# Four attention scores in flight instead of three in the first 60 units, and the bit moves of odd heads placed later

## The chip, the cores and the metric

The kernel runs on one core of one Trainium2 chip. The metric is the time of one execution on the device, in microseconds, the median of the runs; smaller is better. A core has five engines with a queue of instructions each: TensorE (PE in the profile; its weight loads are PEld), VectorE (DVE), ScalarE (ACT), GpSimd (POOL) and SyncE (SP), which issues most of the transfers.

## What is computed

Attention with hashed buckets (4 batches, 8 heads, 768 positions, head dimension 64), and behind it a two-layer network with SiLU on the 3072 tokens (512 to 2048 to 512). Cut to what matters:

```python
q_bits = (einsum('bhsd,dk->bhsk', q, proj) > 0)      # 6 bits; the same for k
mask = q_bucket[:, :, :, None] == k_bucket[:, :, None, :]
scores = where(mask, q @ k.T / 8, -1e9)
attn = exp(scores - max); attn = attn / sum(attn)
x = (attn @ v)  as (3072, 512)
h = x @ w_in; out = (h * sigmoid(h)) @ w_out
```

## The kernel before

The 32 heads are taken as 16 pairs, and a head as nine *units* (`NU`), so there are 288 units. A unit is one score tile of 128 keys by 512 queries, or two halves of 256, in one PSUM bank. Its life: `score(w)` issues one or two matmuls (L381) with K-transposed as weights, ScalarE applies the exponential and writes `u` (L384), and `av(w)` multiplies: four small matmuls (L413) with the parts of `u` as weights and the values `vv` (65 columns, the last of ones, for the row sums) as the moving side. The mask is part of the score: rows 64 to 76 of the operand tiles `QKA` and `QKB` hold the bucket bits (rows 0 to 12 for the odd head), so that the contraction itself puts pairs of unequal buckets far below zero.

Before a pair can be scored it has to be prepared, and for pairs 1 to 5 this is done so:

- `t_unit(p, i)`, i = 0 to 2: four transposes on TensorE into a PSUM tile `tp_ps` (L199), which VectorE copies to `qk32` in SBUF (L201). The third copy completes the pair.
- `cast_unit(p, par)`: GpSimd scales `qk32` into `QKA` (even head) or `QKB` (odd head) in fp16 (L265).
- `proj_halves(p)` (pairs 1 to 3): four projections on TensorE into `bp_ps` (L315), of which VectorE makes `bits` by a comparison (L317).
- `bits_halves(p, par)`: four small moves on VectorE (L332, L335) from `bits` into `QKA` or `QKB`, one for each half of q and of k.

Pairs 4 and 5 use `proj_unit` and `bits_unit` (L295, L301, L359); pair 0 has functions of its own (`t_first`, `proj_first`: L212, L239). `v_unit` prepares the values on GpSimd. At the end of a head VectorE takes the reciprocal of the row sums and scales the output into `x_pr` (L432, L433). `x_unit` transposes `x_pr` to `xT`, by a transfer, or for pairs 2 and 3 on TensorE (L445). The network of the first batch (L478, L488, L491) is mixed in from unit 65 on.

The order of all this is written out by hand. `plan(w, fn)` puts a piece of preparation ahead of unit w, and the main loop runs, for each w: what is planned for w, then pieces of the network if any, then `av(w)`, then `score(w + LEAD)` with `LEAD = 3`. Each engine takes its instructions in this order. So three units are scored ahead of the product that is being issued.

PSUM has eight banks, handed out from rings by tags: "s" with three buffers for scores, "m" with three for transposes, projections and, later, the hidden layer, and "o" with two for the outputs of heads. A new tile of a ring waits until the tile three (or two) turns before it has been read. The pool of `u` has six buffers.

Of the kernel before, what the change touches and what calls it, by code (L numbers as in the profile page):

```python
# [9 lines left out]
F32 = mybir.dt.float32  # L10
# [7 lines left out]
def kernel(  # L18
# [15 lines left out]
    P = 128  # L34
# [23 lines left out]
    ps = ctx.enter_context(tc.tile_pool(name="ps", bufs=1, space=bass.MemoryType.PSUM))  # L58
# [7 lines left out]
    def load_qk(p):  # L66
        b, h0 = p // 4, 2 * (p % 4)
        for n, src in (("q", q), ("k", k)):
            t = ld.tile([P, NJ, 2, D], F32, tag=f"ld{n}", name=f"{n}_sb")
            nc.sync.dma_start(  # L70
                out=t, in_=src[b, h0 : h0 + 2].rearrange("h (p t) d -> p t h d", p=P))
            qk_sb[p, n] = t
# [25 lines left out]
    def load_v(p, heads=slice(0, 2)):  # L98
        b, h0 = p // 4, 2 * (p % 4)
        if p not in v_sb:  # L100
            v_sb[p] = vld.tile([P, 2, NJ * D], F32, tag="ldv", name="v_sb")
        nc.sync.dma_start(
            out=v_sb[p][:, heads],
            in_=v[b, h0 : h0 + 2][heads].rearrange("h (p t) d -> p h (t d)", p=P))
# [87 lines left out]
    def t_unit(p, i):  # L192
        if i == 0:
            qk32[p] = t32.tile([P, 2 * S], F32, tag="qk32", name="qk32")
        tp = ps.tile([P, 512], F32, tag="m", name="tp_ps", bufs=3)
        for j in range(4):
            n, t = divmod(4 * i + j, NJ)
            src = qk_sb[p, "qk"[n]]
            nc.tensor.transpose(tp[:, j * P : (j + 1) * P],  # L199
                                src[:, t].rearrange("p h d -> p (h d)"), ident)  # L200
        nc.vector.tensor_copy(out=qk32[p][:, 512 * i : 512 * (i + 1)], in_=tp)  # L201
# [60 lines left out]
    def cast_unit(p, par):  # L262
        sl = p % NSL
        dst, rows = ((QKA[sl], slice(0, 64)), (QKB[sl], slice(64, 128)))[par]
        nc.gpsimd.tensor_scalar(out=dst[rows, :], in0=qk32[p][rows, :],  # L265
                                scalar1=CS, scalar2=1.0,
                                op0=ALU.mult, op1=ALU.mult)

    def v_unit(p, heads=(0, 1)):
        for i in heads:  # L270
            h = 2 * p + i
            vv, vs = VV[h % NVS], VS[p % (NVS // 2)]
            src = v_sb[p][:, i, :].rearrange("p (t d) -> p t d", d=D)
            nc.gpsimd.tensor_copy(out=vv[:, :, 0:D], in_=src)  # L274
            sa = nrm.tile([P, 3, D], F32, tag="vsa", name="vsa")
            nc.gpsimd.tensor_tensor(out=sa, in0=src[:, 0:3], in1=src[:, 3:6], op=ALU.add)  # L276
            sb = nrm.tile([P, D], F32, tag="vsb", name="vsb")
            nc.gpsimd.tensor_tensor(out=sb, in0=sa[:, 0], in1=sa[:, 1], op=ALU.add)
            nc.gpsimd.tensor_tensor(out=vs[:, i, 0:D], in0=sb, in1=sa[:, 2], op=ALU.add)
# [27 lines left out]
    def proj_halves(p):  # L307


        bt = btp.tile([P, 3, P + 2], F16, tag="bits", name="bits")  # L310
        bp = ps.tile([P, 512], F32, tag="m", name="bp_ps", bufs=3)
        for c in range(4):
            half, n = divmod(c, 2)
            x0 = n * S + half * HS
            nc.tensor.matmul(bp[32 * c : 32 * c + 32, 0:HS], pw[:, 0:32],  # L315
                             qk32[p][:, x0 : x0 + HS], start=True, stop=True)
        nc.vector.tensor_scalar(out=bt[:, :, 0:P],  # L317
                                in0=bp[:, 0:HS].rearrange("d (x c) -> d x c", c=P),
                                scalar1=sc[:, 0:1], scalar2=sc[:, 1:2],
                                op0=ALU.is_gt, op1=ALU.subtract)  # L320
        bits[p] = bt

    def bits_halves(p, par):
        t, r0 = ((QKA[p % NSL], 64), (QKB[p % NSL], 0))[par]
        for c in range(4):
            half, n = divmod(c, 2)
            x0 = n * S + half * HS
            nr = NR if par else NBIT + 1
            r = slice(32 * c, 32 * c + nr)
            dst = t[r0 : r0 + nr, x0 : x0 + HS].rearrange("d (x c) -> d x c", c=P)  # L330
            if n == 1 and par == 1:
                nc.vector.tensor_scalar(out=dst, in0=bits[p][r, :, 0:P],  # L332
                                        scalar1=sc[r, 2:3], scalar2=None, op0=ALU.mult)
            else:
                nc.vector.tensor_copy(out=dst, in_=bits[p][r, :, 0:P])  # L335
# [27 lines left out]

    NU = 9
    LEAD = 3
    ut = {}

    def parts(w):
        h, r = divmod(w, NU)
        jp, j = divmod(r, 3)  # L370
        if j == 1:
            return h, [(2 * jp, 512, 256, 0), (2 * jp + 1, 512, 256, 256)]
        return h, [(2 * jp + j // 2, 0, 512, 0)]

    def score(w):
        h, pts = parts(w)
        p, par = divmod(h, 2)
        t = QKA[p % NSL] if par == 0 else QKB[p % NSL]
        sp = ps.tile([P, 512], F32, tag="s", name="s_ps", bufs=LEAD)
        for jt, c0, n, o0 in pts:  # L380
            nc.tensor.matmul(sp[:, o0 : o0 + n], t[:, S + jt * P : S + (jt + 1) * P],  # L381
                             t[:, c0 : c0 + n], start=True, stop=True)
        u = upl.tile([P, 512], F16, tag="u", name="u")
        nc.scalar.activation(out=u, in_=sp, func=AF.Exp, scale=ESC)  # L384
        ut[w] = u
# [68 lines left out]
    def flush():  # L454
        for fn in after:
            fn()
        after.clear()
# [150 lines left out]
    def moe_head():  # L608
        order = [0, 1, 2, 3, 6, 4] if len(late) == 13 else range(min(6, len(late)))
        units = [late[i] for i in order]  # L610
        late[:] = [u for i, u in enumerate(late) if i not in order]
        return units
# [221 lines left out]
    NW = NH * NU  # L834
# [32 lines left out]
    def plan(w, fn):  # L867
        at.setdefault(w, []).append(fn)
# [2 lines left out]
    plan(1, second_head)  # L871
    plan(3, lambda: nc.gpsimd.memset(QKA[2][64:128, :], 0.0))
    for i in range(3):
        plan(4 + 2 * i, lambda i=i: t_unit(1, i))
    for i in range(2):
        plan(8, lambda i=i: cast_unit(1, i))
        plan(8, lambda i=i: v_unit(1, (i,)))
    plan(10, lambda: proj_halves(1))
    for i in range(2):
        plan(11 + i, lambda i=i: bits_halves(1, i))  # L880
        plan(0, lambda p=2 + i: load_qk(p))
        plan(3 + i, lambda p=2 + i: load_v(p))

    for p, steps, wp in ((2, (14, 17, 20), 24), (3, (28, 31, 34), 41)):
        for i in range(3):
            plan(steps[i], lambda p=p, i=i: t_unit(p, i))
        for par in range(2):
            plan(steps[2], lambda p=p, par=par: cast_unit(p, par))
            plan(wp + 1 + 2 * par, lambda p=p, par=par: bits_halves(p, par))
        plan(wp, lambda p=p: proj_halves(p))  # L890
    for i in range(2):
        for j in range(2):
            plan(18 + 9 * i + 2 * j, lambda p=2 + i, j=j: v_unit(p, (j,)))
        plan(21 + i, lambda p=4 + i: load_qk(p))
# [10 lines left out]
    for Q in range(2, NQUAD):  # L905
# [8 lines left out]
        wp = w0 + {3: 24, 4: 24, 2: 24}.get(Q, 20)  # L914
# [26 lines left out]
    credit = 0.0  # L941
    scoring = True
    in_head = False
    for w in range(LEAD):
        score(w)
    for w in range(NW):
        flush()
        for fn in at.pop(w, []):
            fn()
        if w % BST == 1:  # L950
            moeq.extend(moe_head())
        if w == BST + 5 or w % BST == 11 and w > 2 * BST:
            credit = 0.5
            moeq.extend(moe_list(w // BST - 1))
        keep = 3 if w >= NW - 12 else 0
        left = BST - w % BST
        n = -(-(len(moeq) - keep) // left) if len(moeq) > keep else 0
        in_head = w > 2 * BST and w % BST < 11 or w >= NW - 20
        ahead = BST + 9 < w < 2 * BST
        credit += max(len(moeq) + ahead - keep, 0) / left  # L960
        skip = credit < 0.999 or w % QST in ((20, 21) if w > 2 * BST else (24, 25))
        if w > 2 * BST and w % BST < 11:
            skip = w % BST in (0, 2, 5, 7, 10)
        if n == 1 and len(moeq) - keep < left and skip:
            n = 0
        credit -= n
        if w == BST + 9:
            n = 1
        for _ in range(n):
            moeq.popleft()()  # L970
        av(w)
        if w + LEAD < NW:
            score(w + LEAD)
    while moeq:
        flush()
        moeq.popleft()()
# [35 lines left out]
```

The softmax here doesn't subtract the row's maximum and nothing guards it: scores larger than these inputs give would overflow.

## Time and profile before

| | |
|---|---|
| time, median of 3 runs | 292.36 us (292.26 to 292.48) |
| span of the profiled execution | 290.9 us |
| TensorE busy | 286.3 us, 98% |
| ScalarE busy | 224.5 us, 77% |
| GpSimd busy | 209.4 us, 72% |
| VectorE busy | 201.9 us, 69% |
| first score | 8.79 us |
| product of unit 59 | 42.52 us |

A line of the timeline reads: start, duration, engine, line of the code, operation, out<-in by tile names, how many instructions are merged in it, and in brackets the idle time before it with what ended it. In lists of waits the first number is the total in us, then how often, then the longest. `QKA` is `qka` in the profile and `bp_ps`, `tp_ps`, `s_ps` and `o_ps` are the PSUM tiles. Units up to 59, where the change works, are the first 43 us.

### The profile page before, as it was taken

The numbers are of one execution on the slowest core, as the hardware profiler recorded it, in microseconds if no ns is written. First come the engines' busy times: TensorE is split into PE (matmuls) and PEld (weight loads), VectorE is DVE, ScalarE is ACT, GpSimd is POOL, SyncE is SP. The second block draws the span as 40 slices with busy tenths as digits, with TensorE's granted clock in tenths as the row PEclk, the third lists the DMA queues.
The fourth block names the chain that finished last, engine by engine and source line by source line (L and its number), as shares of the span: only waits on it lengthen the run. The fifth ranks groups of instructions, "written<-read, shape, count | busy, mean of one in ns | idle before, by whom it ended". The sixth has DMA issues, their size and how long they took to land.

```text
span 290.9 us, 7761 instructions
## 1 busy us (share of the span) xinstructions
PE 286.3 (98%) x2934; PEld 196.8 (68%) x2934; DVE 201.9 (69%) x402; ACT 224.5 (77%) x428; POOL 209.4 (72%) x243
## 2 busy tenths in 40 slices
PE   8999999999999999999999999999999999999995
PEld 3676775555667655567666888656668887666885
DVE  5888879899968564855798447975556758777333
ACT  5899998998988686877887877877888865888400
POOL 8779999478998975999357992579999762654400
PEclk9999999999999999999999999999999999999999
DMA  7999997959989439882189325313120211201114
GB/s 201 244 253 193 206 151 121 232 93 179 175 129 206 99 66 195 185 161 54 48 187 125 66 68 114 107 46 38 37 47 0 65 23 60 75 3 36 38 66 134
DMA packets 105861, 32.91 MB, mean 113 GB/s; under 512 B 90912, under 2 KB 105312, under 8 KB 105824
## 3 DMA queue, kind: packets, MB, share of 16 engines
q1 hardware_dynamic: 101296, 28.13, 48.3%
q0 software_dynamic: 4224, 4.19, 9.5%
q8 instruction: 23, 0.38, 0.6%
q10 hardware_dynamic: 304, 0.10, 0.1%
q14 instruction: 14, 0.11, 0.1%
HBM read 27.27 MB, written 6.29 MB: 115 GB/s over the span
## 4 chain that ended last, share of the span: by engine, by line
PE 96%; ACT 2%; issue 1%; DVE 0%; POOL 0%; DVEq 0%; ACTq 0%; POOLq 0%
PE h_ps L478 21%; PE s_ps L381 20%; PE o_ps L530 15%; PE o_ps L413 13%; PE h_ps L689 6%; PE o_ps L796 6%; PE o_ps L560 5%; PE bp_ps L295 3%; ACT u L384 2%; PE tp_ps L199 2%; PE warm_ps L125 1%; PE bp_ps L315 1%; PE tp_ps L212 1%; PE bp_ps L239 1%; PE o_ps L404 0%
## 5 line engine op out<-in xcount | busy, mean ns | idle before, releaser
L384 ACT ACTIVATE u<-s_ps 128x512 f16<-128x512 f32 x288 | 157.4, 612 | 27.1 <-PE s_ps L381 26.8
L413 PEld LDWEIGHTS <-u 128*128 128x128 f16 x1152 | 67.2, 98 | 38.2 <-ACT u L384 9.7
L413 PE MATMUL o_ps<-vv,u 128*128 128x65 f16 x1152 | 82.4, 194 | 0.3
L478 PE MATMUL h_ps<-xT,win 128*128 128x512 f16 (+1 forms) x384 | 75.1, 326 | 0.0
L491 DVE SCALAR_TENSOR_TENSOR g<-th,h_ps 128x512 f16<-128x512 f32 x72 | 48.4, 680 | 36.6 <-ACT th L488 36.1
L381 PE MATMUL s_ps<-qkb 128*128 128x512 f16 x192 | 53.0, 326 | 0.0
L381 PE MATMUL s_ps<-qka 128*128 128x512 f16 x192 | 52.6, 326 | 0.1
L488 ACT ACTIVATE th<-h_ps 128x512 f32<-128x512 f32 x72 | 44.4, 617 | 10.3 <-PE h_ps L478 7.1
L478 PEld LDWEIGHTS <-win 128*128 128x128 f16 x384 | 37.5, 98 | 17.9
L530 PEld LDWEIGHTS <-g 128*128 128x128 f16 x336 | 32.8, 98 | 6.8
L433 POOL TENSOR_TENSOR x_pr<-osum,rec 128x384 f16<-128x384 f32 x23 | 20.0, 872 | 21.6 <-DVE rec L432 20.4
L265 POOL TENSOR_SCALAR qka<-qk 64x1536 f16<-64x1536 f32 x15 | 21.9, 1463 | 14.9 <-DVE qk L260 11.5
L265 POOL TENSOR_SCALAR qkb<-qk 64x1536 f16<-64x1536 f32 x15 | 22.0, 1469 | 1.2
L530 PE MATMUL o_ps<-wt,g 128*128 128x256 f16 x168 | 21.8, 273 | 0.0
L530 PE MATMUL o_ps<-wout,g 128*128 128x256 f16 x168 | 21.4, 273 | 0.0
L513 POOL TENSOR_TENSOR g<-g 128x1024 f16<-128x1024 f16 x7 | 15.2, 2192 | 7.8 <-PE o_ps L530 7.8
L276 POOL TENSOR_TENSOR vsa<-v_sb 128x192 f32<-128x192 f32 x32 | 18.9, 590 | 0.0
L274 POOL CAST vv<-v_sb 128x384 f16<-128x384 f32 x32 | 16.7, 521 | 0.5
L560 PE MATMUL o_ps<-wout,g 128*128 128x512 f16 x64 | 16.4, 379 | 0.0
L703 DVE TENSOR_TENSOR part<-h_ps,part 128x384 f32<-128x384 f32 x24 | 12.6, 554 | 5.1 <-PE h_ps L689 3.0
L260 DVE STREAM_TRANSPOSE qk<-k_blk 128x768 f32<-128x768 f32 x10 | 15.9, 1587 | 0.0
L381 PEld LDWEIGHTS <-qka 128*128 128x128 f16 x192 | 15.4, 97 | 0.7 <-ACT qka L252 0.5
(122 smaller groups left out, 436.6 us busy)
## 6 DMA issues: line engine op xcount, KB each, us to landing
v_sb<-in_v_dram SPq DMA_DIRECT2D x15, 384.0 KB
out_dram<-osb SPq DMA_DIRECT2D x16, 256.0 KB
q_blk<-in_q_dram SPq DMA_DIRECT2D x40, 96.0 KB
k_blk<-in_k_dram SPq DMA_DIRECT2D x40, 96.0 KB
win<-in_moe_w_in_dram POOLq DMA_DIRECT2D x4, 512.0 KB, 7.6
wout<-in_moe_w_out_dram POOLq DMA_DIRECT2D x4, 512.0 KB, 6.7
q_sb<-in_q_dram SPq DMA_DIRECT2D x5, 384.0 KB
k_sb<-in_k_dram SPq DMA_DIRECT2D x5, 384.0 KB
```

The costliest lines, as they stand in the source:

```text
L265: nc.gpsimd.tensor_scalar(out=dst[rows, :], in0=qk32[p][rows, :], scalar1=CS, scalar2=1.0, op0=ALU.mult, op1=ALU.mult)
L276: nc.gpsimd.tensor_tensor(out=sa, in0=src[:, 0:3], in1=src[:, 3:6], op=ALU.add)
L381: nc.tensor.matmul(sp[:, o0 : o0 + n], t[:, S + jt * P : S + (jt + 1) * P], t[:, c0 : c0 + n], start=True, stop=True)
L384: nc.scalar.activation(out=u, in_=sp, func=AF.Exp, scale=ESC)
L413: nc.tensor.matmul(o_ps[h][:, c0 // P + i, :], u[:, o0 + i * P : o0 + (i + 1) * P], vv[:, jt, :], start=(not direct(h) and w % NU == 0 and ...
L433: (nc.vector if direct(h) else nc.gpsimd).tensor_tensor(out=x_pr[p][:, :, par * D : (par + 1) * D], in0=o[:, 0:NJ, 0:D], in1=rec[:, :, Non ...
L478: nc.tensor.matmul(hp[:, :, j, :], w_in16[:, dt, ft * P : (ft + 1) * P], xT[4 * b + dt][:, c0 : c0 + n] .rearrange("d (r c) -> d r c", r=2 ...
L488: nc.scalar.activation(out=th, in_=hp, func=AF.Tanh, scale=0.5)
L491: nc.vector.scalar_tensor_tensor(out=g, in0=th.rearrange("p r f c -> p r (f c)"), scalar=1.0, in1=hp.rearrange("p r f c -> p r (f c)"), op ...
L530: nc.tensor.matmul(op[:, t, :], x[:, k, t * P : (t + 1) * P], y[:, k], start=(first and k == 0), stop=True, skip_group_check=True)
L560: nc.tensor.matmul(op, x, w_out16[:, ft, :], start=(ft == 0), stop=(ft == NFT - 1))
L689: nc.tensor.matmul(bank[i, f], w, x, start=(first and dt == 0), stop=True, skip_group_check=True)
```

## The change

It has four parts.

- The lead is four instead of three for units 0 to 59 (`FOUR`): four scores stand ahead of the loop, and in the loop `score` runs up to w + 4. At w = 5 and w = 14 nothing is scored and two scores follow a step later: units 9 and 18, the first of heads 1 and 2, are left for then. At w = 56 nothing is scored, and from then on the lead is three as before.
- There is no free PSUM bank for the fourth score, so every fourth unit (w % 4 == 1) up to 57 takes its tile from the ring "m" of the transposes.
- Pair 1 is prepared about a unit sooner: its transposes at 4, 5 and 7 instead of 4, 6 and 8, its first cast at 7 instead of 8, its projections at 9 instead of 10, the bits of its even head at 10 instead of 11.
- The bit moves of the odd heads of pairs 1 to 3 are split in two halves of two moves, planned at 15 and 18 (pair 1, before: 12), 32 and 35 (pair 2, before: 27), 45 and 48 (pair 3, before: 44). So they follow copies of transposes of the next pairs in VectorE's queue that they were ahead of before.

No work is added or left out on any engine.

```diff
--- before.py
+++ after.py
@@ -320,9 +320,9 @@
                                 op0=ALU.is_gt, op1=ALU.subtract)
         bits[p] = bt
 
-    def bits_halves(p, par):
+    def bits_halves(p, par, cs=range(4)):
         t, r0 = ((QKA[p % NSL], 64), (QKB[p % NSL], 0))[par]
-        for c in range(4):
+        for c in cs:
             half, n = divmod(c, 2)
             x0 = n * S + half * HS
             nr = NR if par else NBIT + 1
@@ -363,6 +363,7 @@
 
     NU = 9
     LEAD = 3
+    FOUR = 60
     ut = {}
 
     def parts(w):
@@ -376,7 +377,8 @@
         h, pts = parts(w)
         p, par = divmod(h, 2)
         t = QKA[p % NSL] if par == 0 else QKB[p % NSL]
-        sp = ps.tile([P, 512], F32, tag="s", name="s_ps", bufs=LEAD)
+        sp = ps.tile([P, 512], F32, tag="m" if w < FOUR and w % 4 == 1 else "s", name="s_ps",
+                     bufs=3)
         for jt, c0, n, o0 in pts:
             nc.tensor.matmul(sp[:, o0 : o0 + n], t[:, S + jt * P : S + (jt + 1) * P],
                              t[:, c0 : c0 + n], start=True, stop=True)
@@ -871,23 +873,25 @@
     plan(1, second_head)
     plan(3, lambda: nc.gpsimd.memset(QKA[2][64:128, :], 0.0))
     for i in range(3):
-        plan(4 + 2 * i, lambda i=i: t_unit(1, i))
+        plan((4, 5, 7)[i], lambda i=i: t_unit(1, i))
     for i in range(2):
-        plan(8, lambda i=i: cast_unit(1, i))
+        plan(7 + i, lambda i=i: cast_unit(1, i))
         plan(8, lambda i=i: v_unit(1, (i,)))
-    plan(10, lambda: proj_halves(1))
+    plan(9, lambda: proj_halves(1))
+    plan(10, lambda: bits_halves(1, 0))
     for i in range(2):
-        plan(11 + i, lambda i=i: bits_halves(1, i))
+        plan(15 + 3 * i, lambda i=i: bits_halves(1, 1, (2 * i, 2 * i + 1)))
         plan(0, lambda p=2 + i: load_qk(p))
         plan(3 + i, lambda p=2 + i: load_v(p))
 
-    for p, steps, wp in ((2, (14, 17, 20), 24), (3, (28, 31, 34), 41)):
+    for p, steps, wp, wb in ((2, (14, 17, 20), 24, (32, 35)), (3, (28, 31, 34), 41, (45, 48))):
         for i in range(3):
             plan(steps[i], lambda p=p, i=i: t_unit(p, i))
         for par in range(2):
             plan(steps[2], lambda p=p, par=par: cast_unit(p, par))
-            plan(wp + 1 + 2 * par, lambda p=p, par=par: bits_halves(p, par))
+            plan(wb[par], lambda p=p, par=par: bits_halves(p, 1, (2 * par, 2 * par + 1)))
         plan(wp, lambda p=p: proj_halves(p))
+        plan(wp + 1, lambda p=p: bits_halves(p, 0))
     for i in range(2):
         for j in range(2):
             plan(18 + 9 * i + 2 * j, lambda p=2 + i, j=j: v_unit(p, (j,)))
@@ -941,8 +945,9 @@
     credit = 0.0
     scoring = True
     in_head = False
-    for w in range(LEAD):
+    for w in range(LEAD + 1):
         score(w)
+    scored = LEAD + 1
     for w in range(NW):
         flush()
         for fn in at.pop(w, []):
@@ -969,8 +974,10 @@
         for _ in range(n):
             moeq.popleft()()
         av(w)
-        if w + LEAD < NW:
-            score(w + LEAD)
+        early = scored < FOUR and (w, scored) not in ((5, 9), (14, 18))
+        while scored < min(w + LEAD + 1 + early, NW):
+            score(scored)
+            scored += 1
     while moeq:
         flush()
         moeq.popleft()()
```

## The prediction

> **What bounds the kernel now.** I read the page first: the busy shares, the chain, then the waits of the stretch that the change touches (9 to 48 us), and at last the timeline of single instructions there.
>
> ```profile
> PE   8999999999999999999999999999999999999995
> PE 96%; ACT 2%; issue 1%; DVE 0%; POOL 0%; DVEq 0%; ACTq 0%; POOLq 0%
> ```
>
> TensorE is on the chain for 96% of the span, so a microsecond comes off the end only where TensorE itself stops waiting. "9" in every slice does not say that it never waits: the ends of matmuls are modelled. I therefore measure from the start of one matmul to the start of the next.
>
> The waits from 9 to 48 us (total us, times, longest), and then the timeline of ScalarE:
>
> ```profile
> PEld L413 <- ACT u L384: 6.6, 18, 0.6
> ACT u L384 <- PE s_ps L381: 3.3, 6, 1.1
> ```
>
> ```profile
> 9.20 2.06 ACT L384 ACTIVATE u<-s_ps 128x512 f16<-128x512 f32 x4 [0.25 <-PE s_ps L381]
> 11.64 4.84 ACT L384 ACTIVATE u<-s_ps 128x512 f16<-128x512 f32 x9 [0.37 <-PE s_ps L381]
> 17.12 7.19 ACT L384 ACTIVATE u<-s_ps 128x512 f16<-128x512 f32 x14 [0.64 <-PE s_ps L381]
> 24.80 8.96 ACT L384 ACTIVATE u<-s_ps 128x512 f16<-128x512 f32 x17 [0.49 <-PE s_ps L381]
> 34.24 9.64 ACT L384 ACTIVATE u<-s_ps 128x512 f16<-128x512 f32 x19 [0.48 <-PE s_ps L381]
> ```
>
> The two engines wait for each other. A block of transposes or of projections (L199, L315) puts TensorE behind; ScalarE uses up its three finished scores and idles (0.37, 0.64, 0.49, 0.48 us). Afterwards ScalarE is late, and TensorE waits at the next product with `u` (L413). The 6.6 us are idle time of the weight loads, most of it while a matmul still ran. What TensorE lost is seen in its timeline:
>
> ```profile
> 9.44 0.33 PE L404 MATMUL o_ps<-vs,dmat 128*128 128x390 f16 x1
> 9.86 0.24 PE L413 MATMUL o_ps<-vv,u 128*128 128x65 f16 x2
> ...
> 16.98 0.38 PE L381 MATMUL s_ps<-qkb 128*128 128x512 f16 x1
> 17.20 0.28 PE L413 MATMUL o_ps<-vv,u 128*128 128x65 f16 x4
> 17.32 0.38 PE L381 MATMUL s_ps<-qkb 128*128 128x512 f16 x1
> 17.77 0.20 PE L413 MATMUL o_ps<-vv,u 128*128 128x65 f16 x1
> ...
> 22.45 0.38 PE L381 MATMUL s_ps<-qka 128*128 128x256 f16 x2
> 22.90 0.29 PE L413 MATMUL o_ps<-vv,u 128*128 128x65 f16 x4
> ```
>
> An undisturbed score takes 16.98 to 17.20, 0.22 us; four products 17.20 to 17.32, 0.12; so a unit 0.34. The score of 17.32 should be followed at 17.53 but is at 17.77: 0.24 us lost. The same subtraction over this timeline gives the losses before a product: 0.25 at 9.44 (L404 costs 0.17 elsewhere), 0.24 at 17.32, 0.24 at 22.45, 0.07 at 25.22, 0.14 at 26.73, 0.10 at 38.63, 0.07 at 40.81 and 0.16 at 41.12. The sum is 1.26 us. A cross-check: 61 scores at 0.215, 58 times four products at 0.12, 60 transposes at 0.11, four blocks of projections at 0.88, seven L404 at 0.17 and six transposes of `x_pr` at 0.055 make 31.7 us, and they fill 9.2 to 42.3, 33.1 us. So some 1.3 us is all that this stretch can give; ScalarE's idle time is no second prize.
>
> **What the Trainium skill says.** "Perfetto Trace Analysis", section Tensor Engine Instruction: the end of a matmul in a profile is computed from its size, not observed. The trace agrees: rows of 0.38 us follow each other every 0.22. "TensorE: Matmul & The Clock Gate", section Back-to-back issue gap: N/2.4 + 2.5 ns in isolation, 216 ns for 512 columns; here 215. "PSUM — Partial Sum Buffer", section Specifications: eight banks. The pools take three for scores ("s"), three for transposes and projections ("m"), two for outputs: none is free, which is why the fourth score must borrow. Same page, section Engine vs sequencer instructions: ScalarE and VectorE take instructions strictly in order and matmuls start in order; so a product waiting for `u` holds the transposes and scores behind it, and bit moves on VectorE hold the copies behind them (the trace has the copy of the transposes of 18.12 at 20.80, behind eight moves).
>
> **The change part by part.** *Four in flight.* No instruction is added: each score up to unit 59 stands one product earlier. ScalarE then has one more finished score, 0.48 us of work (the first four exponentials span 2.06 us: three steps of 0.48 and a last one of 0.6). The gaps of 0.37, 0.64, 0.49 and 0.48 shrink to about nothing, ScalarE no longer falls behind, and the waits go. The first one goes because score 3 (0.215) now stands in the 0.25. For the others I check that `u` comes first: unit 30's exponential followed score 27, which stood behind the projections (24.33); it now stands ahead of them, and the exponentials start 0.6 us or more sooner against 0.14 lost. At 38 to 42 ScalarE gains 0.5, TensorE needs 0.33. Removed: 1.26. From w = 56 no score is issued for one step, so the lead falls back to three and the extra score isn't a gain by itself. The 1.10 us idle of ScalarE before 44.98, and the waits that follow it until 53 us, stay: unit 60 and on have three.
>
> *Borrowed bank.* Every fourth score takes a turn in the ring of three "m" buffers. Each turn waits for the user three turns back. By the order of the changed program the closest cases are: third transpose of pair 1 behind the copy of its first (ends 13.97, TensorE there at 14.0); score 25 behind the copy of pair 2's second (about 21.0, needed 21.9); score 37 behind the first of pair 3 (about 27.7, needed 28.3). I take 0; bound 0.1 each.
>
> *Pair 1 sooner.* Third transpose at about 14.03 instead of 14.34; VectorE copies it (0.69) until about 15.36 instead of 15.67. But the projections stand a unit sooner: TensorE reaches them at 15.24 instead of 15.71, having skipped a product and 0.25 of wait. Three of the four need that copy: wait 0.15. Behind it stand product 9 and all after, but ScalarE has four scores then. The bits of the even head: `bits` started at 17.15, 0.46 after its projections' end was known, for no reason that the profile shows. Bounds for it now 16.3 to 16.8; four moves of 0.37; score 18 needs three of them, at 18.1 to 18.7, and TensorE is there at 18.68. New wait 0 to 0.05.
>
> *Odd moves later and in halves.* Same eight instructions for a pair, 0.34 to 0.40 each, no change of VectorE's sum. It ran without a gap from 17.15 to 23.36 and again from 33.77 to 41.32, so only order matters:
>
> ```profile
> 17.15 0.68 DVE L317 TENSOR_SCALAR bits<-bp_ps,sc 128x384 f16<-128x384 f32 x1 [0.78 <-PE s_ps L381]
> 17.86 1.45 DVE L335 COPY qka<-bits 7x384 f16<-7x384 f16 x4
> 20.80 1.27 DVE L201 COPY qk<-tp_ps 128x512 f32<-128x512 f32 x2
> 22.68 0.68 DVE L201 COPY qk<-tp_ps 128x512 f32<-128x512 f32 x1
> 24.32 0.68 DVE L317 TENSOR_SCALAR bits<-bp_ps,sc 128x384 f16<-128x384 f32 x1 [0.96 <-PE bp_ps L315]
> ```
>
> The first copy of pair 2 now stands ahead of the odd moves (about 19.0 instead of 20.8), which frees the "m" bank. Score 27 needs the odd bits at about 22.6; they are done at 22.4. The last copy still ends the run: 23.36 less 0.31, 23.05; TensorE reaches the projections of pair 2 at 22.98. Wait 0 to 0.1; with score 18, I take 0.05. For pair 3 the run to 41.32 ends with the `x_pr` that the transposes at 41.84 need; it starts only 0.5 sooner, at about 33.25, so `x_pr` is ready at 40.85 where TensorE would be at 40.77: 0.12. GpSimd, also nearly full, gets pair 1's cast 0.3 sooner; its products are not needed within 2 us.
>
> Sum: 1.26 - 0.15 - 0.05 - 0.12 = 0.94. From 53 us TensorE runs without such waits until 100, and in all loses below 0.8 us from 100 to 200, so what is won at 42 us arrives at the end: 292.36 - 0.94 = 291.42.
>
> **Rivals.** *A: VectorE takes over the wait.* For: it is gapless in two runs, and projections and `xt_ps` already sit just behind its copies. If the unexplained 0.46 stays and the copies come no sooner than before, the three new waits are 0.3, 0.3 and 0.3 and the gain is 0.35: 292.0. Against: pair 1's copy does come 0.3 sooner.
> *B: won, then lost.* The loads keep the DMA engines full until 53 us and the queue of SyncE never rests from 20 to 52; something due at a fixed time (blocks of pair 6, read at 52.57) could stop the earlier TensorE. Against: all inputs of the first 60 units landed 1 us or more ahead, and no matmul waits for a load after 9 us. It would give 292.2.
> *C: slower.* The ring of "m" ties scores to VectorE's copies, and late odd bits or score 18 stop TensorE. Each such stop is one VectorE operation, 0.35 to 0.69; four of them at 0.47 are 1.9 against the 1.26 regained, +0.6: 293.0. Against: the margins above, 0.2 to 0.9 us where a score waits on the ring.
>
> **How the numbers follow.** The forecast, gain over 0.58 us: 0.71, among it a few hundredths where the new waits vanish as well (1.26 and a little: 291.0). A 0.12 and B 0.07 fall within 0.2%: 0.19. C: 0.10. The range 290.9 to 292.6 holds the forecast, both bounds of the waits, A and B, and the better half of the step to C.
>
> **What would show it.** Right: ScalarE's gaps before 17.1, 24.8 and 34.2 shrink below 0.2; the eight losses before products vanish; the projections of pair 1 start at about 15.3; score 62 and the projections of unit 60 come at about 42.0 instead of 42.95; the same shift stands at 100 us and at the end; the 1.10 gap before unit 63 remains. Wrong: scores with a wait on a VectorE copy, the projections of pair 2 later than 23.2, or a shift at 43 us that is gone at 100.

## The result and the profile after

The changed kernel takes 291.14 us (median of 6 runs, 290.99 to 291.51) where the kernel before takes 292.15 in the same comparison (291.88 to 292.48): ratio 0.9967, 95% interval 0.9954 to 0.9980. The medians are 1.0 us apart; 291.4 was predicted.

The executions of one and the same kernel spread over some 0.7 to 1 us (a few come later still): in the 14 profiled executions the first score comes at 8.03 to 8.98 us (more on this at the end). In every one of these the time is 1.77 to 1.87 us plus the end of the last instruction, so an early or late start shifts the time as it is. I therefore also compare kernels by the distance from the first score to the end in the trace, in which this start drops out: 282.10 us before, 281.23 after. This gain of 0.87 us is what the change is worth; the rest of the 1.0 is how the starts of the runs fell. A second profile of the changed kernel on another occasion gave 281.20; in this one case the measure repeated within 0.03.

The line of the page on the chain, after the change (the row of busy tenths is the same as before):

```profile
PE 98%; DVE 1%; ACT 0%; issue 0%; POOL 0%; DVEq 0%; ACTq 0%; POOLq 0%
```

TensorE still bounds the kernel. ScalarE has gone from the chain (2% to 0%), and VectorE has come onto it with 1%. The waits from 9 to 48 us:

```profile
PEld L415 <- ACT u L386: 4.0, 11, 0.6
ACT u L386 <- PE s_ps L383: 3.4, 6, 1.1
```

The lines are two further down in the code (L413 is L415, L381 is L383, L384 is L386). The weight loads wait 4.0 us for `u` instead of 6.6; as before, most of that passes while a matmul still runs. In TensorE's timeline the product of unit 13, which stood at 17.77 after a loss of 0.24, now follows the score ahead of it at once, 0.22 us from start to start:

```profile
17.02 0.38 PE L383 MATMUL s_ps<-qkb 128*128 128x256 f16 x2
17.24 0.29 PE L415 MATMUL o_ps<-vv,u 128*128 128x65 f16 x4
```

ScalarE waits as long for scores as before. Its timeline:

```profile
8.67 4.54 ACT L386 ACTIVATE u<-s_ps 128x512 f16<-128x512 f32 x9 [0.25 <-PE s_ps L383]
13.51 2.16 ACT L386 ACTIVATE u<-s_ps 128x512 f16<-128x512 f32 x4 [0.30 <-PE s_ps L383]
16.48 7.45 ACT L386 ACTIVATE u<-s_ps 128x512 f16<-128x512 f32 x15 [0.82 <-PE s_ps L383]
24.48 8.44 ACT L386 ACTIVATE u<-s_ps 128x512 f16<-128x512 f32 x17 [0.54 <-PE s_ps L383]
33.33 9.11 ACT L386 ACTIVATE u<-s_ps 128x512 f16<-128x512 f32 x18 [0.41 <-PE s_ps L383]
43.56 4.03 ACT L386 ACTIVATE u<-s_ps 128x512 f16<-128x512 f32 x8 [1.12 <-PE s_ps L383]
```

The idle times in brackets have not shrunk (0.82, 0.54 and 0.41 where 0.64, 0.49 and 0.48 stood). So these idle times were not what cost the time. What counts is whether TensorE waits for `u`, and up to unit 59 it hardly does any more (0.03 us, ahead of the first product). The following table accounts for this. It adds up, for every matmul from the first score to the product of unit 60, the time from its start to the next one's, by the line in the kernel before:

```
line, what                     before    after   difference, us
L381  scores                   15.093   14.205   -0.888
L404  first product of a head   1.500    1.232   -0.268
L413  products with u           7.466    7.349   -0.117
L315  projections, pairs 1-3    2.430    2.754   +0.324
L199  transposes                6.548    6.602   +0.054
L445  transposes of x_pr        0.335    0.345   +0.010
L239, L295 projections          2.215    2.215    0
sum                            35.587   34.702   -0.885
```

A wait ahead of a product appears in the line of what stands before it, so the first three rows are the waits for `u`. They also hold a new wait of 0.053 ahead of the transposes of `x_pr`. So 1.33 us went and 0.44 came. (The eight waits are 1.25 of it, less the 0.03 that is left; most of the other 0.1 lies within the products, where first steps of 0.038 us have become 0.029.) The shift is 0.89 at the product of unit 60. In the two profiles of the changed kernel it is 0.88 and 0.89 at unit 100 (63.53 us from the first score before, 62.65 and 62.64 after) and 0.87 and 0.89 at the last unit, 287 (227.77 before, 226.90 and 226.88 after): next to nothing is lost later.

Where the 0.44 us come from is read on VectorE. Its timeline after:

```profile
16.34 0.68 DVE L317 TENSOR_SCALAR bits<-bp_ps,sc 128x384 f16<-128x384 f32 x1 [0.78 <-PE bp_ps L315]
17.05 1.46 DVE L335 COPY qka<-bits 7x384 f16<-7x384 f16 x4
18.54 0.69 DVE L201 COPY qk<-tp_ps 128x512 f32<-128x512 f32 x1
19.26 0.34 DVE L335 COPY qkb<-bits 13x384 f16<-13x384 f16 x1
...
22.05 0.67 DVE L201 COPY qk<-tp_ps 128x512 f32<-128x512 f32 x1
23.68 0.68 DVE L317 TENSOR_SCALAR bits<-bp_ps,sc 128x384 f16<-128x384 f32 x1 [0.96 <-PE bp_ps L315]
```

The first copy of pair 2 stands at 18.54, ahead of the odd moves, as planned. The run without a gap is 6.38 us long, 16.34 to 22.72, where it was 6.21 us before (17.15 to 23.36). TensorE's timeline meanwhile:

```profile
22.54 1.08 PE L315 MATMUL bp_ps<-qk,pw 128*32 128x384 f32 x8
23.55 0.29 PE L415 MATMUL o_ps<-vv,u 128*128 128x65 f16 x4
```

The projections of pair 2 stand from 22.54 to 23.55, 1.01 us; they took 0.855 before, and take 0.78 where nothing holds them (pair 3). Two of the four need the copy that ends at 22.72. The projections of pair 1 take 0.955 us instead of 0.79 for the same reason.

### The profile page after: what moved, and what is told of

It is laid out like the page before. It is cut to its first block, busy times and chain, and to the rows that moved or that the text cites. A ratio compares the mean times of both kernels' runs of the same rounds, so it can differ in the third digit from the quotient of the medians.

```text
span 289.5 us, 7762 instructions
## 1 busy us (share of the span) xinstructions
PE 285.0 (98%) x2934; PEld 197.2 (68%) x2934; DVE 202.1 (70%) x402; ACT 223.8 (77%) x428; POOL 209.6 (72%) x243
## 4 chain that ended last, share of the span: by engine, by line
PE 98%; DVE 1%; ACT 0%; issue 0%; POOL 0%; DVEq 0%; ACTq 0%; POOLq 0%
PE h_ps L480 22%; PE s_ps L383 22%; PE o_ps L532 15%; PE o_ps L415 13%; PE h_ps L691 6%; PE o_ps L798 6%; PE o_ps L562 5%; PE bp_ps L295 3%; PE tp_ps L199 2%; PE warm_ps L125 1%; PE bp_ps L315 1%; PE bp_ps L239 1%; PE o_ps L406 1%; PE tp_ps L212 1%; PE xt_ps L447 0%; DVE qka L252 0%
## 5 line engine op out<-in xcount | busy, mean ns | idle before, releaser
L386 ACT ACTIVATE u<-s_ps 128x512 f16<-128x512 f32 x288 | 156.5, 618 | 27.1 <-PE s_ps L383 27.0
L415 PEld LDWEIGHTS <-u 128*128 128x128 f16 x1152 | 67.7, 98 | 35.4 <-ACT u L386 6.4
L415 PE MATMUL o_ps<-vv,u 128*128 128x65 f16 x1152 | 81.8, 194 | 0.1
L383 PE MATMUL s_ps<-qkb 128*128 128x512 f16 x192 | 52.7, 326 | 0.0
L383 PE MATMUL s_ps<-qka 128*128 128x512 f16 x192 | 52.1, 326 | 0.2 <-DVE qka L252 0.2
L383 PEld LDWEIGHTS <-qka 128*128 128x128 f16 x192 | 15.4, 97 | 0.9 <-ACT qka L252 0.6
```

The lines of the kernel that those rows point to most:

```text
L415: nc.tensor.matmul(o_ps[h][:, c0 // P + i, :], u[:, o0 + i * P : o0 + (i + 1) * P], vv[:, jt, :], start=(not direct(h) and w % NU == 0 and ...
```

## The experiments

Every run is timed against the kernel before on the same chip. "From the first score" is the distance explained above: 282.10 us in the kernel before, 281.20 in the changed kernel's run below. The ratios still contain the spread of the starts, so small differences are read from the last column.

| run | ratio to before (95%) | from the first score |
|---|---|---|
| changed kernel | 0.9964 (0.9949 to 0.9980) | 281.20 |
| four in flight alone | 1.0015 (1.0003 to 1.0026) | 282.80 |
| new places alone | 1.0001 (0.9988 to 1.0013) | 282.30 |
| odd moves early | 1.0011 (1.0001 to 1.0021) | 282.52 |
| odd moves late, whole | 0.9991 (0.9982 to 1.0001) | 281.59 |
| pair 1 as before | 0.9974 (0.9961 to 0.9987) | 281.49 |
| four up to unit 63 | 0.9964 (0.9951 to 0.9978) | 281.36 |
| four up to unit 67 | 0.9977 (0.9967 to 0.9987) | 281.35 |
| own buffer for pair 1's bits | 0.9951 (0.9938 to 0.9964) | 280.95 |
| own buffer, up to 63, `x_pr` at 77 | 0.9968 (0.9959 to 0.9978) | 281.20 |
| own buffer, `x_pr` at 77 | 0.9972 (0.9963 to 0.9981) | 281.15 |
| kernel before, own buffer | 1.0006 (0.9994 to 1.0018) | 282.01 |

The changed kernel once more, as the base of the others:

> The changed kernel again, as the yardstick of this set. Theory (the waits for u in the first 60 units are gone, less what waits for VectorE's copies took back): ratio to before 0.9965 to 0.9975, and in its profile the product of unit 60 lies 0.8 to 1.0 us nearer to score 0 than in the kernel before (33.1 to 33.4 us against 34.1 between them... counted from score 0 to the product of unit 60: 35.59 us before). Rival (a good start only: score 0 came 0.53 us sooner in the profile of after): then the distance from score 0 to the end is the same in both.

Measured: 0.9964, the result repeated. The product of unit 60 comes 34.70 us behind the first score instead of 35.59, so it is not a good start only.

**Four in flight, with the old places of everything else.**

```diff
-        plan((4, 5, 7)[i], lambda i=i: t_unit(1, i))
+        plan(4 + 2 * i, lambda i=i: t_unit(1, i))
...
-        plan(15 + 3 * i, lambda i=i: bits_halves(1, 1, (2 * i, 2 * i + 1)))
+        plan(12, lambda i=i: bits_halves(1, 1, (2 * i, 2 * i + 1)))
-    for p, steps, wp, wb in ((2, (14, 17, 20), 24, (32, 35)), (3, (28, 31, 34), 41, (45, 48))):
+    for p, steps, wp, wb in ((2, (14, 17, 20), 24, (27, 27)), (3, (28, 31, 34), 41, (44, 44))):
```

(and cast, projections and even bits of pair 1 at 8, 10 and 11)

> Four scores in flight and the borrowed bank, with the old plan of pair 1 and of the odd bit moves. My theory: the lead takes the waits for u away, but VectorE's copies of pairs 2 and 3 now come too late for the ring m (score 25 behind the copy of pair 2's second transposes: about 0.4 us; score 37 behind pair 3's first: up to 1.0) and for the projections of pair 2 (0.4): most of the 1.26 is given back, gain 0 to 0.4 us, ratio 0.9985 to 1.000, and scores show waits for VectorE. Rival 1 (the lead is all of it): ratio 0.9967 as the whole change. Rival 2 (the plan is all of it): ratio 1.000 with the eight waits for u still there.

Measured: slower than before, by 0.70 us from the first score. The theory had the kind of loss right, but neither its size nor its places. The waits from 8 to 43 us:

```profile
PEld L415 <- ACT u L386: 2.8, 5, 0.6
...
PEld tp_ps L199 <- DVE qk L201: 1.3, 2, 1.0
```

The eight waits for `u` are gone here as well; transposes that wait for a copy by VectorE have come. By single matmuls: score 18 waits 0.45 us for the even bits, transposes at 20.5 wait 0.15 and 0.06, the third transposes of pair 3 0.85 and score 53 0.57 for a copy. That is 2.07 us against 1.33 regained, +0.74; measured +0.70.

**The new places, with three in flight.**

```diff
-    FOUR = 60
+    FOUR = 0
-    for w in range(LEAD + 1):
+    for w in range(LEAD):
-    scored = LEAD + 1
+    scored = LEAD
-        while scored < min(w + LEAD + 1 + early, NW):
+        while scored < min(w + LEAD + 1, NW):
```

> Pair 1 a unit sooner and the odd moves later and in halves, with three scores in flight and no borrowed bank. My theory: the waits for u stay, ScalarE still idles 0.4 to 0.6 us after each block of projections: ratio 0.9995 to 1.0005, perhaps 0.1 us slower as the projections of pair 1 wait for their copy. Rival 2 (the plan is all of it): 0.9967. Rival 1: 1.000.

Measured: no gain; the ratio is 1.0001, and from the first score it is 0.20 us slower. Nine waits for `u` are there, 0.25, 0.23, 0.14, 0.24, 0.06, 0.14, 0.10, 0.07 and 0.16, 1.39 us in sum. The moves and pair 1's earlier place win nothing by themselves: alone, the parts give +0.70 and +0.20 us from the first score, together -0.90.

**Which move matters: the odd bits early.** The changed kernel, with the odd moves where they were.

```diff
-        plan(15 + 3 * i, lambda i=i: bits_halves(1, 1, (2 * i, 2 * i + 1)))
+        plan(12, lambda i=i: bits_halves(1, 1, (2 * i, 2 * i + 1)))
-    for p, steps, wp, wb in ((2, (14, 17, 20), 24, (32, 35)), (3, (28, 31, 34), 41, (45, 48))):
+    for p, steps, wp, wb in ((2, (14, 17, 20), 24, (27, 27)), (3, (28, 31, 34), 41, (44, 44))):
```

> The change with the odd moves at their old places (12, 27, 44), pair 1 sooner. My theory: as in the run with the lead alone the copies of pairs 2 and 3 stand behind the odd moves, scores 25 and 37 and the projections of pair 2 wait 0.3 to 1.0 us: gain 0.1 to 0.5 us, ratio 0.998 to 0.9997. If the late odd moves do nothing for the time: 0.9967.

Measured: slower than before, by 0.42 us from the first score where a gain of 0.1 to 0.5 was expected, and 1.32 us behind the changed kernel. The waits are not at the places I had named. TensorE, then VectorE, in this kernel:

```profile
27.44 0.38 PE L383 MATMUL s_ps<-qka 128*128 128x256 f16 x2
28.50 0.66 PE L199 MATMUL tp_ps<-ident,k_sb 128*128 128x128 f32 x4 [0.68 <-DVE qk L201]
...
37.05 0.29 PE L415 MATMUL o_ps<-vv,u 128*128 128x65 f16 x4
37.75 0.38 PE L383 MATMUL s_ps<-qkb 128*128 128x512 f16 x1 [0.41 <-DVE qk L201]
```

```profile
26.33 0.33 DVE L335 COPY qkb<-bits 13x384 f16<-13x384 f16 x1
26.68 0.40 DVE L332 TENSOR_SCALAR qkb<-bits,sc 13x384 f16<-13x384 f16 x1
27.09 0.34 DVE L335 COPY qkb<-bits 13x384 f16<-13x384 f16 x1
27.44 0.41 DVE L332 TENSOR_SCALAR qkb<-bits,sc 13x384 f16<-13x384 f16 x1
27.78 1.27 DVE L201 COPY qk<-tp_ps 128x512 f32<-128x512 f32 x2
...
37.03 0.67 DVE L201 COPY qk<-tp_ps 128x512 f32<-128x512 f32 x1
```

Four moves stand in a row from 26.33, 1.45 us, and behind them the copy of pair 3's first transposes. The third transposes, due at 27.66, wait for the bank which that copy frees and start at 28.50: 0.85 lost. The same happens at 37.03: score 53, which has a bank of the same ring, waits 0.57.

It is not the late copy alone that costs this time. In the kernel before, TensorE and VectorE at the same place:

```profile
28.90 0.60 PE L199 MATMUL tp_ps<-ident,k_sb 128*128 128x128 f32 x4
```

```profile
28.75 1.86 DVE L201 COPY qk<-tp_ps 128x512 f32<-128x512 f32 x3
```

There the copy of the first transposes (the first of the three merged here) came just as late, 28.75 to 29.42, and the third transposes started at 28.90 without a wait: no score took turns in the ring. So the borrowed bank is what makes a late copy cost time; with the moves behind the copies it costs next to nothing.

The waits also show that the turns of a ring are not as strict as the description of the kernel before has it. By strict turns score 37 would have had the bank of the first transposes, which is read until 28.45 (the end of the first of the two copies merged at 27.78), but it started at 27.44; the third transposes, a turn later, were the ones that waited for that copy. Which free bank a tile gets, the profile does not show.

**Late, but whole.** The changed kernel, with all four moves of a pair at one place.

```diff
-        plan(15 + 3 * i, lambda i=i: bits_halves(1, 1, (2 * i, 2 * i + 1)))
+        plan(18, lambda i=i: bits_halves(1, 1, (2 * i, 2 * i + 1)))
-    for p, steps, wp, wb in ((2, (14, 17, 20), 24, (32, 35)), (3, (28, 31, 34), 41, (45, 48))):
+    for p, steps, wp, wb in ((2, (14, 17, 20), 24, (35, 35)), (3, (28, 31, 34), 41, (48, 48))):
```

> The changed kernel with the odd bit moves late but not in halves: all four of a pair at 18, 35 and 48. Theory (what counts is that they stand behind the copies of the transposes, not the halves): ratio 0.996 to 0.9972, and the block of projections of pair 2 waits 0 to 0.1 us less, since the copies before it are no longer interleaved with moves. Rival (the halves are needed: four moves in a row stand ahead of a copy or of a score of the odd head): 0.998 or more, with a wait of 0.3 us or more at a score of an odd head (27 or 45) or at a third transpose.

Measured: 0.9991. Seven of its thirteen executions started late, which this ratio contains; from the first score it takes 0.51 us less than the kernel before and 0.39 more than the changed one. That is the rival's side, just, though not at its places. VectorE in this kernel:

```profile
19.09 0.69 DVE L201 COPY qk<-tp_ps 128x512 f32<-128x512 f32 x1
20.22 0.69 DVE L201 COPY qk<-tp_ps 128x512 f32<-128x512 f32 x1 [0.43 <-PE tp_ps L199]
...
21.52 0.33 DVE L335 COPY qkb<-bits 13x384 f16<-13x384 f16 x1
21.86 0.40 DVE L332 TENSOR_SCALAR qkb<-bits,sc 13x384 f16<-13x384 f16 x1
22.30 0.34 DVE L335 COPY qkb<-bits 13x384 f16<-13x384 f16 x1
22.67 0.41 DVE L332 TENSOR_SCALAR qkb<-bits,sc 13x384 f16<-13x384 f16 x1
23.01 0.67 DVE L201 COPY qk<-tp_ps 128x512 f32<-128x512 f32 x1
```

Between the first two copies VectorE now idles 0.43 us, which half of the moves used to fill. All four stand ahead of the third copy, and the block of projections of pair 2 grows from 1.01 to 1.42 us. That 0.41 accounts for the 0.39. The theory missed the gap that one half had filled.

**Pair 1 where it was.**

```diff
-        plan((4, 5, 7)[i], lambda i=i: t_unit(1, i))
+        plan(4 + 2 * i, lambda i=i: t_unit(1, i))
-        plan(7 + i, lambda i=i: cast_unit(1, i))
+        plan(8, lambda i=i: cast_unit(1, i))
-    plan(9, lambda: proj_halves(1))
-    plan(10, lambda: bits_halves(1, 0))
+    plan(10, lambda: proj_halves(1))
+    plan(11, lambda: bits_halves(1, 0))
```

> The change with pair 1 at its old steps (4, 6, 8; casts 8; projections 10; bits 11), four in flight and the late odd moves kept. My theory: score 18 waits for the even head's bits of pair 1, 0.4 to 0.5 us (with the lead alone it waited 0.45), and nothing else new: ratio 0.9975 to 0.9985, 0.3 to 0.5 us behind the whole change. If pair 1's step does nothing: 0.9965.

Measured: 0.29 us behind the changed kernel from the first score. In TensorE's timeline score 18 is what waits, 0.45 us by the starts:

```profile
17.58 0.41 PE L415 MATMUL o_ps<-vv,u 128*128 128x65 f16 x8
18.27 0.59 PE L383 MATMUL s_ps<-qka 128*128 128x512 f16 x3 [0.28 <-DVE qka L335]
```

The projections of pair 2 wait 0.08 us longer too, which the theory did not have. Against this, the waits of pair 1's third transposes and projections (0.06 and 0.17) are gone.

**Four in flight for longer.** `FOUR = 64`, and `FOUR = 68`.

> Four in flight up to unit 63 instead of 59, so that the projections of pairs 4 and 5 at unit 60 also find a fourth score. My theory: the 1.1 us idle of ScalarE before unit 63 shrinks by one exponential, 0.48, and the waits of products from there to unit 75 (0.06 to 0.14 each, 0.58 in all), which come from ScalarE being late, shrink by as much: 0.4 to 0.5 us faster than the whole change, ratio 0.9945 to 0.9955. Rival: from unit 63 on VectorE's moves or the hidden layer hold TensorE: ratio 0.9965.

> Four in flight up to unit 67. Same theory: the stretch up to unit 75 is paced by ScalarE's exponentials at 0.48 us, so a longer lead adds nothing to the one exponential won at unit 60: as four up to 63, within 0.1 us. Rival: units 61 and 65 in the banks of the hidden layer cost a wait of 0.3 us or more, as that layer starts at unit 65.

Measured: neither beats the changed kernel. With 64, unit 63 comes 0.12 us sooner. Then the transposes of `x_pr` ahead of unit 75 wait longer for VectorE:

```profile
50.26 0.38 PE L383 MATMUL s_ps<-qka 128*128 128x512 f16 x1
51.02 0.51 PE L447 MATMUL xt_ps<-ident,x_pr 128*128 128x128 f16 x6 [0.38 <-DVE x_pr L435]
```

From the score to these transposes it takes 0.76 us, where the changed kernel needs 0.40; of the 0.76, 0.55 is waiting (0.57 with 68; 0.19 in the changed kernel). From unit 60 to these transposes VectorE sets the pace. One more score now stands ahead of the projections of unit 60, which start 33.43 us from the first score instead of 33.27. VectorE works without a pause from the comparison behind them (34.57 instead of 34.41) to the `x_pr` that the transposes need (41.98 instead of 41.82). So the same 0.16 us is what the kernel loses, and a TensorE that is ahead in between only waits longer. The runs with 64 and with 68 agree in this.

**The pause ahead of pair 1's bits.** In the kernel before, `bits` of pair 1 started 0.46 us later than the profile explained. It is still so after the change (source view of L317):

```profile
L317 DVE TENSOR_SCALAR bits<-bp_ps,sc x3: 676/677/677, 16.3 to 32.9; 128x384 f16<-128x384 f32 x3
L317 DVEq EVENT_SEMAPHORE  x1: 50/50/50, 15.8 to 15.8; - x1
```

Only one of the three comparisons has a wait instruction of its own ahead of it, and this one starts 0.51 us after it. The Trainium skill, "Perfetto Trace Analysis", section Identifying Dependency Chains, says that an instruction which waits on several engines may have such an instruction inserted before it. The trace agrees: the instruction waits for TensorE and ScalarE, and the comparison itself for GpSimd. The buffer of pair 1's bits is one that pair 0's moves have read, and those were shared out among VectorE, ScalarE and GpSimd. With a buffer that nobody has read before, the comparison waits for TensorE alone:

```diff
-        bt = btp.tile([P, 3, P + 2], F16, tag="bits", name="bits")
+        bt = (ops.tile([P, 3, P + 2], F16, tag="osb", name="bits", bufs=3) if p == 1 else
+              btp.tile([P, 3, P + 2], F16, tag="bits", name="bits"))
```

> The change with the bits of pair 1 in a buffer of their own kind (one of the output buffers, unused then), so that their comparison waits for TensorE alone and no longer for the old readers on ScalarE and GpSimd, which finished 7 us before. Theory: the 0.46 us between the separate wait instruction and the comparison (both kernels have it) belongs to that wait instruction; it goes, VectorE's run starts 0.4 us sooner and the projections of pair 2 lose their 0.24 us wait: 0.1 to 0.25 us faster than the whole change, ratio 0.9957 to 0.9962. Rival: the pause has another cause: it stays, ratio 0.9965.

Measured: 0.9951, and 0.25 us less than the changed kernel from the first score. This beats both kernels. The time's interval overlaps that of the changed kernel, and by their times (290.78 to 290.92) its five executions all started early, so the 0.25 us of the trace is the better figure. VectorE:

```profile
15.64 0.68 DVE L318 TENSOR_SCALAR bits<-bp_ps,sc 128x384 f16<-128x384 f32 x1 [0.26 <-PE bp_ps L316]
...
21.62 0.67 DVE L201 COPY qk<-tp_ps 128x512 f32<-128x512 f32 x1
23.26 0.68 DVE L318 TENSOR_SCALAR bits<-bp_ps,sc 128x384 f16<-128x384 f32 x1 [0.97 <-PE bp_ps L316]
```

The idle time before the comparison is 0.26 instead of 0.78. The copies behind it come sooner, and the projections of pair 2 take 0.78 us instead of 1.01: their wait is gone.

**The same buffer in the kernel before** (the edit above, applied to it).

> The kernel before with nothing but the own buffer for the bits of pair 1. Theory (VectorE's pause before the comparison costs time only where VectorE is what TensorE waits for, and in the kernel before that is u): the pause of 0.5 us goes, the eight waits for u stay, ratio 0.9995 to 1.0005. Rival (the pause costs the same 0.3 us in either kernel): 0.9985 to 0.999.

Measured: 1.0006, as the theory had it. The comparison starts 0.27 us after VectorE fell idle, and all eight waits for `u` stay, 1.25 us in sum. From the first score the gain is 0.09 us, most of it at the projections of pair 2, which take 0.785 us instead of 0.855. So the pause costs far less here than the 0.25 us that it costs in the changed kernel.

**Both ideas, with the late transposes moved.** `FOUR = 64` with the own buffer, and the transposes of `x_pr` two units later; then the later place without the 64.

```diff
-        plan((30, 42, 58, 75)[p] if p < 4 else 2 * NU * (p + 1) + (2 if p % 4 == 3 else 9),
+        plan((30, 42, 58, 77)[p] if p < 4 else 2 * NU * (p + 1) + (2 if p % 4 == 3 else 9),
```

> The changed kernel with the own buffer for the bits of pair 1, the fourth score kept up to unit 63, and the first transposes of x_pr on TensorE two units later (77 instead of 75). Theory (what took the gain of the run with 64 was only the place of those transposes: they stood 0.545 us waiting for VectorE): two units later the wait is at most 0.1, and the waits for u behind unit 63 that four scores avoid stay away, so 0.3 to 0.5 us less than with the own buffer alone, ratio to the kernel before 0.9935 to 0.9942. Rival (TensorE between units 60 and 80 waits for VectorE one way or the other, at the transposes or at the hidden layer that needs their copy): within 0.15 us of the own buffer alone, ratio 0.9946 to 0.9956.

> As the run before, but with the fourth score only up to unit 59: control. If the later place alone is worth something, it is the 0.05 to 0.18 us that the transposes of x_pr waited in the changed kernel: ratio 0.9945 to 0.9951. If it costs (the hidden layer needs the copy sooner than it then comes), 0.9955 or more.

Measured: 0.25 and 0.20 us more from the first score than the own buffer alone. The theory fell; the rival had the place, the hidden layer, but thought the loss smaller. That layer needs the copy `xT`, and the wait moves on to it. In the run with 64, TensorE and VectorE:

```profile
50.87 0.38 PE L384 MATMUL s_ps<-qka 128*128 128x512 f16 x1
51.83 0.38 PE L481 MATMUL h_ps<-xT,win 128*128 128x512 f16 x1 [0.58 <-DVE xT L449]
```

```profile
49.83 1.56 DVE L260 STREAM_TRANSPOSE qk<-q_blk 128x768 f32<-128x768 f32 x1
51.25 0.53 DVE L449 COPY xT<-xt_ps 128x768 f16<-128x768 f16 x1
```

Two units later the copy stands behind a transpose of 1.56 us in VectorE's queue, which it was ahead of before. The hidden layer loses 0.75 us there, and 0.48 in the control. Whether four in flight pay beyond unit 59 with both of these out of the way was not tried.

## Why the prediction was right

- **The eight waits for `u` go, 1.26.** Right: they were 1.25, and 0.03 is left, ahead of the first product. With what goes inside the products the table has 1.33 removed. The run with the new places alone keeps these waits, so it is the fourth score that removes them.
- **ScalarE's gaps shrink to about nothing.** Wrong. The gaps stayed (0.82, 0.54, 0.41) and TensorE's waits went all the same. ScalarE's first 63 exponentials, up to the gap before unit 63, took 33.77 us less 2.07 of shown gaps, 0.503 each; before, 34.68 less 1.98, 0.519. It made up its time in short stalls that the merged lines do not show: against its undisturbed step of 0.48 us from start to start, those of less than 0.2 us each add up to 1.6 us before and 0.6 after. The step took the gaps as the cause of the later lateness, and they need not be. The first sign of being right, gaps below 0.2, did not come true.
- **Ring "m" costs 0.** Nearly: the third transposes of pair 1 wait 0.055, within its bound of 0.1. The run with the odd moves early shows what the margin rests on. With the moves at their old places it costs 0.85 and 0.57 us, at pair 3's third transposes and score 53, not at scores 25 and 37. The places came from counting three turns back, and that count failed for score 37.
- **Projections of pair 1, 0.15.** Measured 0.165; they start at 15.29, counted as if the first score came at 8.79 (predicted 15.3). Only two of the four need the third copy, not three; the wait is the same, as the second of them is one of the two.
- **Score 18 and projections of pair 2, 0.05 together.** Score 18 waits 0. The projections wait 0.16 more than before, the cost that was missed by most. I let VectorE's run keep its length and start 0.31 sooner. It started 0.27 sooner by the same count (16.88 against 17.15) and grew by 0.17.
- **Transposes of `x_pr`, 0.12.** Measured 0.05.
- **Sum 0.94, carried to the end.** 0.885 from the first score to unit 60, 0.87 to 0.89 at the end. That the sum is so close is in part luck: 0.07 more went than counted, and 0.44 came instead of 0.32. The measured 291.14 lies below 291.42 because the kernel before ran at 292.15 in this comparison, not at 292.36, and because the starts fell well. The projections of unit 60 start at 42.06 by the same count (predicted 42.0), and the gap before unit 63 is 1.12.
- **The rivals.** A is true in kind: VectorE took back 0.44 of 1.33, not 0.9. B did not happen. C is what the fourth score does with everything else at its old place: 1.0015, with 2.07 us of stops where C reckoned with 1.9. With the odd moves alone put back it is 1.0011.

## What to carry to other kernels

A deeper queue between two engines that borrows its buffers pays if a third engine frees them in time: here the depth and the new places each cost time alone (0.7 and 0.2 us), and won 0.9 together. Look for losses in the starts of the engine that bounds the kernel, not in the idle time of the one that it waits for; the two did not go together here. When moving work in a queue, ask which gap it filled where it was, and what it now stands behind.

## What the runs showed of the hardware

- The comparison with a wait instruction of its own started 0.45 to 0.47 us after the end of that instruction, in all ten profiles that have one; with one engine to wait for, in the other four, the pause was gone. A copy that waits for the same three engines in the same way lost only 0.04 us (own buffer, at 18.12), so it is not a price of every such wait. What makes the difference stays open. In the ten profiles the comparison also starts 0.07 to 0.09 us before GpSimd's cast of pair 1 ends. With the own buffer it starts during that cast, so the cast does not keep VectorE busy; whether the comparison's own wait for GpSimd is what takes the time was not tried apart from the other two.
- The start of the kernel is not steady. In the five profiled executions with the first score at 8.60 us or later, the step from the fourth to the fifth matmul of the first projections (L239) takes 0.62 us, in the nine others at most 0.41. Why is open. In thirteen runs of the kernel with late whole moves the times were 291.38 to 291.56 or 292.01 to 292.40, and nothing between; the ten with the own buffer and `x_pr` at 77 spread over 290.94 to 291.66 without such a gap. A change of 0.3 us is hidden in this spread unless the start is taken out.
